# A transformer block on one core: a region of its own for the down weights, late weights on two DMA queues, smaller first loads, one more slot and a new unit order

## The chip, the cores and the metric

The kernel runs on one core of one Trainium2 chip. The metric is the device time of one execution in microseconds (us), the median of several runs. The engines are named as in the profile: PE (TensorE matmuls; PEld its weight loads), DVE (VectorE), ACT (ScalarE), POOL (GpSimd) and SP (SyncE, which here only issues DMAs). DMAs are issued by SP and by ACT, each into a queue of its own; all of them run on the core's 16 DMA engines.

## The reference

One sequence of S = 2048 rows and D = 640 columns goes through linear attention with a softmax feature map, and then through a bilinear gated MLP (F = 1536). All tensors are bf16.

```python
H, Dh = 32, 20
xn = layernorm(x)
q, k, v = split_heads(xn @ wqkv)                      # each [H, S, 20]
phi = lambda t: concat([softmax(t @ w_phi), softmax(-(t @ w_phi))])   # per head, 40 features
kv  = sum over s of phi(k)[s, f] * v[s, d]            # [H, 40, 20]
z   = sum over s of phi(k)[s, f]
o   = (phi(q) @ kv) / (phi(q) @ z + 1e-6)
h   = x + o @ wo
hn  = layernorm(h)
out = h + ((hn @ w_gate) * (hn @ w_up)) @ w_down
```

## The kernel before

The 2048 rows are 16 tiles of 128 rows, numbered t = 0 to 15. The program is a graph of about a thousand operations, and each of them has a name made of a stage and a tile. These are the stages, in the order in which one tile goes through them:

- `x` loads the rows. `L1s`, `L1a`, `L1l`, `L1e` and `L1n` compute the first layernorm's statistics on DVE, ACT and POOL, and `xn` (DVE or ACT) writes the normalised tile.
- `xt` turns that tile, so that its columns lie on partitions. Tiles 0 to 3 are turned by PE and copied out of PSUM by `xte`; the others by a DMA transpose that SP issues (line 468).
- `V`, `K` and `Q` are the three projections on PE (line 481, 10 matmuls of 320 columns). For tiles 0 and 1 they are split into five units each (`K0_0` to `K0_4`), one for each 128-row chunk of the weight. The feature map w_phi is folded into the K and Q weights first: `WT` turns chunk i of wk on PE (line 389), `WTe` copies it out, `F1_i` multiplies it with w_phi (line 408), and `Fe1_i` copies the result into `Wp`. `wqt` and `F0_i` do the same for wq.
- `Kx` and `Qx` are two exponentials each on ACT (line 493), of the projection and of its negative; `Ks` and `Qs` sum them per head on DVE (line 497); `Kr`, `Ke`, `Qr` and `Qe` form the reciprocals on ACT; `Kn` and `Qn` multiply on POOL (lines 517, 549 and 553).
- `KV` adds the tile's share of kv and z on PE (line 525) in one PSUM group over all 16 tiles. `KVe` copies the sum out when all tiles are in.
- `qT` turns the Q features (11 blocks of 128) by a DMA transpose that SP issues (line 560). `N` multiplies them with kv and z (line 578, 12 matmuls); `dd`, `rd` and `o` divide on DVE.
- `oT` turns the quotient by a DMA transpose on SP (line 598). `O` multiplies it with wo (line 604, 10 matmuls), and `h` adds x on DVE.
- `L2s`, `L2a`, `L2v` and `L2r` are the second layernorm's statistics; `hc` centres the tile on ACT or DVE; `hT` turns it by a DMA transpose on SP (line 631).

The MLP runs over five blocks of rows: 256, 512, 512, 512 and 256. `U b_f_g` multiplies block b with the f-th 128 columns of w_gate (g = 0) or w_up (g = 1), 5 matmuls of 256 or 512 columns (line 646). `g` copies the gate out of PSUM on ACT (line 651), and `u` multiplies it with the up product on DVE (line 654). `D` multiplies with the down weights `Wd` (line 665, 24 matmuls of 320 columns for a tile), `y` adds h on DVE (line 677), and `w` stores the tile (line 679). The last tile's `D` is cut into three column ranges. Ten matmuls on zeros (`warm0` to `warm9`, line 368) come first on PE.

The work's order isn't decided at run time. `PLAN` lists, for each operation, a number to sort by, then a choice of engine (empty or 0: the first of its alternatives, 1: the second), then the slots that its result takes in a rotating buffer: `xn4:17.845::0` is operation `xn4`, sorted at 17.845, on its first engine, into slot 0. `arrange` sorts by that number, and each engine then carries out its own list in order. `emit` places the semaphore waits that the data and the reuse of slots need. An instruction that waits therefore holds up all that stands behind it on its engine, DMA issues included. The figures for duration that `G.op` also takes play no part in the emitted program; only the list does.

The rotating buffers of `NSLOTS` include `ph` (4 slots, Q features before turning), `phT` (5, after), `oT` (4) and `psum` (8 banks). `phT` and `oT` lie in one region, `scratch`, where wk and the turned weights lie earlier.

The weights load as follows. `wk` and `wv` (each five chunks of 128 rows, 160 KB a chunk) come in pieces of 2, 2 and 1 chunks at the start, beside `x`, on both queues. After the last `xt`, SP issues `wg` and `wu` (5 pieces of 384 KB each) and `wo` (320 and 480 KB). The down weights are four pieces `wd0` to `wd3` of 480 KB. Their tile `Wd` lies over `Wp`, which holds the folded K and Q weights and the V weights, so they wait for projections:

```python
    for k in range(4):
        dma("sp", "wd%d" % k, ..., key=310, after=kvprojs if k < 3 else projs)
```

`kvprojs` are all K and V projections and `projs` all projections, Q too. In the emitted order SP issues wd0 to wd2 just before the qT of tile 2, and wd3 after the last Q projection.

Of the kernel before, what the change touches and what calls it, by code (L numbers as in the profile page):

```python
# [6 lines left out]
BF16 = mybir.dt.bfloat16  # L7
# [37 lines left out]
NSLOTS = {"psum": 8, "xn": 4, "ek": 7, "va": 8, "SR": 4, "ph": 4, "phT": 5, "o": 3, "oT": 4, "gt": 4, "hh": 2, "out": 3,  # L45
# [3 lines left out]
x0:1.18 wk0:1.66 wk2:1.18:1 wk4:3.1:1 x1:0.7 wv0:1.66 wv2:2.14 wv4:2.62 x2:2.14:1 x4:2.62 x6:3.1 w5:0.7 x8:3.58:1 x10:4.06 x12:3.58 x14:4.06:1  # L49
wqt0:37.137 wqt1:29.337 wqt2:35.837 wqt3:34.537 wqt4:42.509 wo0:50.109 wo2:52.989 wg0:48.669 wu0:47.709 wg1:48.189 wu1:52.029 wg2:52.509 wu2:49.629  # L50
wg3:49.149 wu3:51.549 wg4:51.069 wu4:50.589 id0:0.7 gl0:1 eps:3.13 id1:1.25 gla0:2.69 glb0:5.289 gla4:2.47 glb4:2.91 gla1:3.55 glb1:3.99 gla2:4.41
glb2:5.509 gla3:3.33 glb3:3.77 va1:1.65 phz:6.843 mk0:4.21 mk1:7.743 mk2:8.143 mk3:8.543 mk4:8.943 zero:0.7 warm0:1.08::0 warm1:1.51 warm2:1.94
warm3:2.37 warm4:2.8 warm5:3.23 warm6:3.66 warm7:4.09 warm8:4.52 warm9:4.74 Ph0:5.729 Ph1:6.388 Ph2:4.63 WT0:7.595::0 WTe0:8.469:1 WT1:7.001::3
WTe1:7.55 WT2:6.404::1 WTe2:7.093:1 WT3:6.125::0 WTe3:6.674 WT4:11.659::4 WTe4:12.387:1 F1_0:9.442::6 Fe1_0:10.534:1 F1_1:9.018::4 Fe1_1:9.911
F1_2:7.874::6 Fe1_2:8.609:1 F1_3:7.28::4 Fe1_3:7.985 F1_4:13.296::4 Fe1_4:13.881:1 L1s0:5.222 L1a0:6.542 L1s1:3.734 L1a1:4.734 L1s2:8.887 L1a2:11.457
L1s3:9.707 L1a3:11.347 L1s4:10.527 L1a4:15.165 L1s5:11.567 L1a5:12.805 L1s6:12.915 L1a6:15.055 L1s7:14.235 L1a7:15.275 L1s8:16.205 L1a8:23.367
L1s9:22.547 L1a9:23.587 L1s10:17.025 L1a10:23.477 L1s11:15.385 L1a11:18.345 L1s12:32.127 L1a12:34.367 L1s13:31.307 L1a13:35.897 L1s14:26.537
L1a14:27.857 L1s15:36.007 L1a15:38.247 L1l0:6.832 L1e0:7.262 L1l1:5.024 L1e1:5.454 L1l2:12.009 L1e2:12.439 L1n2:12.949 L1n3:12.749 L1l4:15.95
L1e4:16.794 L1n4:17.304 L1n5:17.704 L1n6:17.104 L1n7:17.504 L1l8:24.71 L1e8:26.417 L1n8:26.955 L1n9:26.755 L1n10:29.714 L1n11:27.155 L1l12:38.83
L1e12:39.29 L1n12:39.901 L1n13:42.86 L1n14:40.101 L1n15:42.66 xn0:7.969::0 xt0:8.739::1 xte0:9.288 xn1:6.042::0 xt1:6.722::2 xte1:7.362 xn2:13.735::1  # L60
xt2:14.434::1 xte2:15.327 xn3:13.162:1:0 xt3:14.154::0 xte3:14.704 xn4:17.845::0 xt4:18.525 xn5:18.14:1:1 xt5:19.825 xn6:19.477:1:2 xt6:21.125
xn7:19.875::3 xt7:22.425 xn8:29.387::1 xt8:31.937 xn9:27.357::0 xt9:28.037 xn10:30.264:1:3 xt10:33.237 xn11:29.55:1:2 xt11:30.637 xn12:40.529::0
xt12:41.209 xn13:44.357::0 xt13:45.109 xn14:40.557:1:1 xt14:43.809 xn15:43.01:1:2 xt15:46.409 V0_0:10.3::0 V0_1:10.572 V0_2:11.115 V0_3:11.387
V0_4:11.938 Ve0:12.539::1 K0_0:13.024::2 K0_1:13.611 K0_2:14.713 K0_3:14.984 K0_4:15.528 Kx0_0:16.17::0 Kx0_1:17.517 Ks0:18.455::0 Kr0:20.814
Ke0:21.677 Kn0:22.037 KV0:25.308::4,5 V1_0:8.195::2 V1_1:8.467 V1_2:9.757 V1_3:10.029 V1_4:10.844 Ve1:11.385::0 K1_0:12.209::6 K1_1:12.481 K1_2:12.753
K1_3:13.883 K1_4:15.256 Kx1_0:16.894::1 Kx1_1:18.854 Ks1:21.127::1 Kr1:23.074 Ke1:23.937 Kn1:24.396 KV1:29.698 V2:17.158::0 Ve2:20.375:1:3
K2:19.874::6 Kx2_0:21.827::3 Kx2_1:24.087 Ks2:25.117::0 Kr2:27.914 Ke2:29.4 Kn2:29.914 KV2:32.73 V3:15.799::4 Ve3:20.19::2 K3:18.516::2
Kx3_0:21.054::2 Kx3_1:22.45 Ks3:23.697::2 Kr3:25.554 Ke3:26.517 Kn3:27.355 KV3:33.046 V4:21.233::4 Ve4:23.314::4 K4:30.014::0 Kx4_0:32.614::5
Kx4_1:33.477 Ks4:34.477::3 Kr4:37.194 Ke4:38.68 Kn4:40.301 KV4:42.87 V5:22.591::0 Ve5:24.93::5 K5:25.623::6 Kx5_0:27.29::0 Kx5_1:28.154 Ks5:29.887::2
Kr5:31.6 Ke5:32.464 Kn5:32.824 KV5:44.544 V6:26.982::0 Ve6:28.777::1 K6:23.949::2 Kx6_0:25.794::4 Kx6_1:26.667 Ks6:27.967::1 Kr6:33.237 Ke6:34.1  # L70
Kn6:35.183 KV6:44.859 V7:31.372::6 Ve7:34.25::0 K7:28.34::2 Kx7_0:30.977::1 Kx7_1:31.84 Ks7:32.947::0 Kr7:34.874 Ke7:35.737 Kn7:37.542 KV7:45.49
V8:37.436::2 Ve8:39.777:1:3 K8:34.72::0 Kx8_0:36.57::3 Kx8_1:37.434 Ks8:38.357::1 Kr8:39.957 Ke8:40.407 Kn8:43.06 KV8:46.435 V9:40.153::6
Ve9:41.781:1:6 K9:38.795::0 Kx9_0:41.27::6 Kx9_1:42.104 Ks9:42.937::0 Kr9:44.537 Ke9:45.4 Kn9:47.778 KV9:51.456 V10:36.078::6 Ve10:38.057::2
K10:41.511::2 Kx10_0:43.723::5 Kx10_1:44.777 Ks10:45.61::1 Kr10:47.21 Ke10:47.66 Kn10:50.137 KV10:53.673 V11:43.185::0 Ve11:44.857:1:4 K11:33.361::2
Kx11_0:35.114::2 Kx11_1:35.947 Ks11:36.827::2 Kr11:39.05 Ke11:39.5 Kn11:45.419 KV11:54.26 V12:55.119::2 Ve12:56.747:1:0 K12:50.097::6 Kx12_0:51.886::3
Kx12_1:52.719 Ks12:53.637::1 Kr12:55.237 Ke12:56.101 Kn12:57.605 KV12:60.552 V13:57.835::0 Ve13:59.464:1:1 K13:48.424::2 Kx13_0:50.052::1
Kx13_1:50.886 Ks13:52.217::0 Kr13:54.023 Ke13:54.886 Kn13:55.246 KV13:63.584 V14:66.616::6 Ve14:68.977:1:0 K14:46.751::6 Kx14_0:48.379::0
Kx14_1:49.212 Ks14:50.046::2 Kr14:51.646 Ke14:52.509 Kn14:52.869 KV14:70.691 V15:67.975::2 Ve15:69.603::1 K15:56.477::6 Kx15_0:58.105::5 Kx15_1:58.939
Ks15:60.215::0 Kr15:62.279 Ke15:63.142 Kn15:65.048 KV15:71.007 KVe0:71.852 KVe1:71.592 F0_0:45.805::0 Fe0_0:46.39 F0_1:45.175::6 Fe0_1:45.76
F0_2:46.12::2 Fe0_2:47.03:1 F0_3:49.782::0 Fe0_3:51.466:1 F0_4:48.109::0 Fe0_4:48.694:1 Q0_0:51.771::2 Q0_1:52.043 Q0_2:52.314 Q0_3:52.586 Q0_4:52.858  # L80
Qx0_0:53.399::4 Qx0_1:54.263 Qs0:55.096::3 Qr0:56.934 Qe0:57.384 Qn0:59.964::0 qT0:62.656::0 Q1_0:53.129::0 Q1_1:53.401 Q1_2:53.988 Q1_3:54.575
Q1_4:54.847 Qx1_0:55.477::2 Qx1_1:56.311 Qs1:57.499::2 Qr1:59.562 Qe1:60.012 Qn1:62.506::1 qT1:65.198::1 Q2:59.194::2 Qx2_0:60.822::6 Qx2_1:61.655
Qs2:62.489::1 Qr2:64.599 Qe2:65.462 Qn2:67.407::0 qT2:71.043::2 Q3:62.226::6 Qx3_0:63.975::4 Qx3_1:64.839 Qs3:65.672::2 Qr3:67.872 Qe3:68.735
Qn3:69.949::1 qT3:72.641::3 Q4:69.333::0 Qx4_0:70.961::6 Qx4_1:71.939 Qs4:72.772::2 Qr4:74.407 Qe4:75.275 Qn4:77.575::0 qT4:80.683::2 Q5:65.258::0
# [152 lines left out]
def build_graph():  # L237
# [665 lines left out]
```

## Time and profile before

| | |
|---|---|
| median of three runs | 278.77 us (278.11 to 279.57) |
| the profiled execution: time, span | 279.31 us, 277.6 us |
| mean granted TensorE clock | 0.994 |
| PE busy | 267.5 us (96%) |
| DVE, ACT, POOL busy | 169.7 us (61%), 113.4 us (41%), 89.8 us (32%) |
| chain that ended last | PE 86%, DMA 7%, DVE 3% |
| HBM read, written | 11.00 MB, 2.62 MB |

Times in the profile count from the first instruction of the span. The execution's own time is 1.7 us more than its span, and this execution was 0.5 us above the median. In a timeline row the columns are start, duration, engine, line, operation, output and inputs, count, and in brackets how long the engine had been idle before the row and what ended that. A row with a count merges successive instructions of one kind. SPq and ACTq rows are DMA issues, and their duration is that of the issue, not of the transfer; the time from issue to landing stands in the DMA rows, after the size. In a row of the windows view the columns are the window, its length, the busy time of PE, PEld, DVE, ACT and POOL (with the number of instructions), the granted PE clock, the share of the DMA engines' time and GB/s.

### The profile page before, as it was taken

Reading aid. Unit: us, or ns where it says so; the run is one execution under the profiler, and the core shown is the slowest. Engines: PE = TensorE matmul, PEld = TensorE weight load, DVE = VectorE, ACT = ScalarE, POOL = GpSimd, SP = SyncE. Lnnn points to the kernel's source line nnn. Section 1 sums busy time; section 2 is a strip of 40 time slices with the busy share of each in tenths; the row PEclk is TensorE's granted clock in tenths of the full one; section 3 lists DMA queues with packets and bytes.
Section 4 is the critical chain, followed back from the end, with each engine's and each line's share of the span. In section 5 each row is a group of like instructions: output and inputs, shape, how many; then the busy total and the mean of one; then the engine's idle time right before and its main releaser. Section 6 shows DMA issues by size and latency. Waiting matters only on the chain.

```text
span 277.6 us, 5213 instructions
## 1 busy us (share of the span) xinstructions
PE 267.5 (96%) x2119; PEld 178.3 (64%) x2119; DVE 169.7 (61%) x317; ACT 113.4 (41%) x240; POOL 89.8 (32%) x107
## 2 busy tenths in 40 slices
PE   7899999999997799999999999999999999999996
PEld 3777778777765577755556787764545457644775
DVE  4899997888778869896734348950244302505323
ACT  2899998769783534443204032213031300013000
POOL 8017999899968507443000000000000000000000
PEclk9999999999999979999999999999999999999999
DMA  7914545996599989867410003550001001100011
GB/s 225 367 38 86 94 100 103 282 399 128 192 203 171 157 160 176 152 90 137 85 24 0 26 24 50 108 108 24 0 24 20 6 12 50 47 0 0 26 47 61
DMA packets 66520, 27.77 MB, mean 100 GB/s; under 512 B 57664, under 2 KB 65216, under 8 KB 66496
## 3 DMA queue, kind: packets, MB, share of 16 engines
q1 hardware_dynamic: 64704, 25.30, 41.2%
q10 hardware_dynamic: 1792, 2.13, 2.3%
q8 instruction: 17, 0.28, 0.4%
q14 instruction: 7, 0.06, 0.1%
HBM read 11.00 MB, written 2.62 MB: 49 GB/s over the span
## 4 chain that ended last, share of the span: by engine, by line
PE 86%; DMA 7%; DVE 3%; ACT 1%; issue 1%; SPq 0%
PE ps L646 35%; PE ps L481 21%; PE ps L665 19%; PE ps L604 6%; DMA scratch<-o 3%; DMA scratch<-in_A_wqkv_dram 2%; PE ps L525 2%; DVE SR L497 1%; PE ps L578 1%; PE ps L408 1%; DMA xnT<-xn 1%; ACT ek L493 1%; DVE o L594 1%; ACT xn L627 1%; DVE ev L654 0%
## 5 line engine op out<-in xcount | busy, mean ns | idle before, releaser
L646 PE MATMUL ps<-xnT,Wgu 128*128 128x512 bf16 (+1 forms) x600 | 108.0, 340 | 0.6 <-DMA xnT<-xn 0.6
L646 PEld LDWEIGHTS ps<-xnT,Wgu 128*128 128x128 bf16 x600 | 59.3, 99 | 45.7 <-DVE ev L654 1.0
L651 ACT ACTIVATE gt<-ps 128x512 bf16<-128x512 f32 (+1 forms) x60 | 30.5, 512 | 108.0 <-PE ps L646 76.8
L481 PE MATMUL ps<-Wp,xnT 128*128 128x320 bf16 x480 | 68.9, 299 | 0.0
L654 DVE TENSOR_TENSOR ev<-ps,gt 128x512 bf16<-128x512 f32 (+1 forms) x60 | 33.0, 578 | 49.4 <-ACT gt L651 19.0
L481 PEld LDWEIGHTS ps<-Wp,xnT 128*128 128x128 bf16 x480 | 45.6, 98 | 16.6
L665 PE MATMUL ps<-Wp,ev 128*128 128x320 bf16 (+2 forms) x396 | 53.2, 295 | 0.0
L493 ACT ACTIVATE ek<-ps 128x640 bf16<-128x640 f32 x64 | 43.4, 701 | 11.1 <-PE ps L481 11.0
L497 DVE TENSOR_REDUCE SR<-ek 128x64 f32<-128x1280 bf16 x32 | 46.7, 1468 | 2.0 <-ACT ek L493 1.4
L665 PEld LDWEIGHTS ps<-Wp,ev 128*128 128x128 bf16 x396 | 38.1, 98 | 14.6 <-issue 0.2
L549 POOL TENSOR_TENSOR ph<-ek,SR 128x1200 bf16<-128x1200 bf16 x16 | 35.5, 2222 | 16.8 <-ACT SR L502 12.7
L517 POOL TENSOR_TENSOR ek<-ek,SR 128x1280 bf16<-128x1280 bf16 x16 | 37.4, 2360 | 5.2 <-ACT SR L502 5.2
L677 DVE SCALAR_TENSOR_TENSOR Wp<-ps,rs,x_all 128x640 bf16<-128x640 f32 (+3 forms) x18 | 14.6, 809 | 31.5 <-PE ps L665 31.4
L618 POOL TENSOR_SCALAR ln<-mv 128x1 f32<-128x1 f32 x16 | 3.3, 210 | 90.0 <-DVE mv L617 89.7
L604 PE MATMUL ps<-Wo,scratch 128*128 128x320 bf16 x160 | 24.1, 299 | 2.5 <-DMA scratch<-o 2.5
L604 PEld LDWEIGHTS ps<-Wo,scratch 128*128 128x128 bf16 x160 | 15.2, 98 | 9.1 <-DMA scratch<-o 3.6
L608 DVE TENSOR_TENSOR x_all<-ps,x_all 128x640 bf16<-128x640 f32 x16 | 13.1, 817 | 5.1 <-PE ps L604 5.0
L594 DVE TENSOR_TENSOR o<-ps,sm 128x640 bf16<-128x640 f32 x16 | 12.9, 815 | 2.8 <-DMA scratch<-o 2.6
L627 ACT ACTIVATE xn<-x_all,mv 128x640 bf16<-128x640 bf16 x12 | 9.9, 825 | 11.1 <-DVE mv L617 10.7
L500 ACT ACTIVATE SR<-SR 128x64 f32<-128x64 f32 x32 | 8.2, 256 | 5.3 <-DVE SR L497 5.3
L578 PE MATMUL ps<-KVm,scratch 128*128 128x63 bf16 x192 | 7.8, 189 | 2.1 <-DMA scratch<-ph 2.1
L578 PEld LDWEIGHTS ps<-KVm,scratch 128*128 128x128 bf16 x192 | 7.3, 98 | 3.7 <-DMA scratch<-ph 2.5
(52 smaller groups left out, 148.9 us busy)
## 6 DMA issues: line engine op xcount, KB each, us to landing
out_dram<-Wp SPq DMA_DIRECT2D x15, 160.0 KB, 1.8
Wgu<-in_B_w_up_dram SPq DMA_DIRECT2D x5, 384.0 KB, 7.6
Wgu<-in_B_w_gate_dram SPq DMA_DIRECT2D x5, 384.0 KB, 6.2
Wp<-in_B_w_down_dram SPq DMA_DIRECT2D x4, 480.0 KB, 5.2
x_all<-in_A_x_dram SPq DMA_DIRECT2D x5, 320.0 KB, 10.1
Wp<-in_A_wqkv_dram ACTq DMA_DIRECT2D x2, 320.0 KB, 6.2
x_all<-in_A_x_dram ACTq DMA_DIRECT2D x2, 320.0 KB, 9.6
Wo<-in_A_wo_dram SPq DMA_DIRECT2D x1, 480.0 KB, 8.9
```

What stands on the lines that cost most here:

```text
L481: ins = e.matmul(pb(b, hb)[:, 0:320], lhsT=T["xnT"][:, NC - 1 - c, P * t:P * (t + 1)], rhs=T["Wp"][:, POS[kind], c, 320 * hb:320 * (hb + 1 ...
L493: G.op("act", "%sx%d_%d" % (nm, t, s), lambda e, s=s, b=b, ek=ek: e.activation(out=T["ek"][:, ek.slots[0], :].rearrange("p (b h s f) -> p ...
L497: G.op("dve", "%ss%d" % (nm, t), lambda e, ek=ek, sr=sr: e.tensor_reduce(out=T["SR"][:, sr.slots[0], 0, :], in_=T["ek"][:, ek.slots[0], :] ...
L517: G.op("pool", "Kn%d" % t, lambda e, ek=ek, sr=sr: e.tensor_tensor(out=T["ek"][:, ek.slots[0], :].rearrange("p (h f) -> p h f", f=DH), in0 ...
L549: e.tensor_tensor(out=o_[:, 0:10 * P].rearrange("p (g n) -> p g n", n=P)[:, :, 0:120].rearrange("p g (h f) -> p g h f", f=DH), in0=i_[:, 0 ...
L578: ins = e.matmul(pb(b, y)[:, 21 * (h0 - 16 * y):21 * (h1 - 16 * y)], lhsT=T["phT"][:, phT.slots[0], g, :], rhs=T["KVm"][:, h0:h1, :].rearr ...
L594: G.op("dve", "o%d" % t, lambda e, sm=sm, b=b, o=o: e.tensor_tensor(out=T["o"][:, o.slots[0], :].rearrange("p (b h d) -> p b h d", b=2, d= ...
L604: ins = e.matmul(pb(b, hb)[:, 0:320], lhsT=T["oT"][:, oT.slots[0], c, :], rhs=T["Wo"][:, c, 320 * hb:320 * (hb + 1)], start=(c == 0), stop ...
L646: ins = e.matmul(pb(b)[:, 0:n], lhsT=T["Wgu"][:, gu, c, P * ft:P * (ft + 1)], rhs=T["xnT"][:, NC - 1 - c, o0:o0 + n], start=(c == 0), stop ...
L651: G.op("act", "g%d_%d" % (bi, ft), lambda e, pg=pg, gt=gt, n=n: e.activation(out=T["gt"][:, gt.slots[0], 0:n], in_=pb(pg)[:, 0:n], func=AF ...
L654: o_ = G.op("dve", "u%d_%d" % (bi, ft), lambda e, pu=pu, gt=gt, hh=hh, ft=ft, n=n: e.tensor_tensor(out=T["hh"][:, hh.slots[0], ft, 0:n], i ...
L665: ins = e.matmul(pb(b, hb)[:, 0:w], lhsT=T["hh"][:, hh.slots[0], ft, P * tt:P * (tt + 1)], rhs=T["Wd"][:, ft, c0 + w * hb:c0 + w * (hb + 1 ...
```

## The change

- `Wd` gets a region of its own (15,360 bytes a partition); the three `out` slots move to the start of `Wp`. The loads wd0 to wd3 then wait for nothing, and they stand among the other late weights in the list.
- The late weights `wo`, `wg`, `wu` and `wd` may go out on SP or ACT. In the new list `wg1`, `wu2` and `wd0` are on ACT.
- `wk` and `wv` load in single chunks of 160 KB, and tiles 2 and 3 of x load one by one. At the start ACT has w5, wk0, wk2, wk4, x3, wv0, wv2 and wv4, between its first activations; SP has x0, wk1, x1, x2, wk3, wv1, x4, wv3, x6 and so on.
- `phT` has six slots instead of five.
- The list is new from end to end: the order on every engine, the choices of engine and the slots. The operations and their shapes are otherwise the same.

Parts of the new order, as read from the list:

| | before | after |
|---|---|---|
| PE, head | WT3 WT2 xt1 WT1 F1_3 WT0 F1_2 V1_0 V1_1 xt0 F1_1 F1_0 ... | WT0 WT1 xt0 WT2 F1_0 F1_1 WT3 F1_2 WT4 K0_0 K0_1 F1_3 V0_0 ... |
| SP, late weights | xt12 wqt4 xt14 xt13 xt15, then wu0 to wo2 | xt15 wg0 xt13 wo0 wu1 wu4 wo2 wd3 xt14 wu3 wg3 wu0 wg2 wd2 wg4 wd1 |
| POOL, Q features | Qn0 Qn1 Kn15 Qn2 Qn3 Qn15 Qn5 Qn4 Qn6 Qn9 ... | Qn1 Qn3 Qn0 Kn14 Qn2 Qn5 Qn6 Qn4 Qn15 Qn9 ... |
| SP, middle | qT0 qT1 wd0 wd1 wd2 qT2 qT3 qT15 oT1 qT5 oT0 qT4 oT2 qT6 oT3 qT9 hT1 hT0 ... | qT1 qT3 qT0 qT2 qT5 oT1 oT0 qT6 qT4 oT2 qT15 oT3 qT9 hT1 hT0 ... |
| PE, middle | N1 Q9 N0 Q8 Q10 Q11 N2 N3 Q7 O1 O0 N5 Q13 O2 Q12 N6 N15 O3 N4 N9, then U0 | N1 N0 Q11 Q12 Q13 N2 Q14 N3 Q10 O1 O0 N5 Q8 N6 O2 Q7 N15 O3 N9 N4, then U0 |
| PE, first D | after U1 and N12, beside U4 | D0 and D1 between U0 and U1 |

```diff
-NSLOTS = {"psum": 8, "xn": 4, "ek": 7, "va": 8, "SR": 4, "ph": 4, "phT": 5, ...
+NSLOTS = {"psum": 8, "xn": 4, "ek": 7, "va": 8, "SR": 4, "ph": 4, "phT": 6, ...
 PLAN = {}
-x0:1.18 wk0:1.66 wk2:1.18:1 wk4:3.1:1 x1:0.7 wv0:1.66 wv2:2.14 wv4:2.62 x2:2.14:1 x4:2.62 x6:3.1 w5:0.7 x8:3.58:1 ...
+x0:0.7 w5:1.18:1 wk0:1.66:1 wv0:5.98:1 wk1:2.14 wv1:5.5 wk2:3.1:1 wv2:6.46:1 wk3:4.06 wv3:7.9 wk4:4.54:1 wv4:7.42:1 ...
...
-    xload("sp", 0, 1, -100)
-    for n_, (a, b_) in enumerate(((0, 2), (2, 4), (4, 5))):
-        dma("sp", "wk%d" % a, lambda a=a, b_=b_: T["wkn"][:, a:b_, :], ...
-        dma("act", "wv%d" % a, lambda a=a, b_=b_: T["Wp"][:, POS[2], a:b_, :], ...
+    for c in range(NC):
+        for k_, nm, dst, bf, kk in ((1, "wk", lambda c: T["wkn"][:, c, :], wkn_b, 1.0), (2, "wv", lambda c: T["Wp"][:, POS[2], c, :], wp_b[2], 2.8)):
+            dma("act" if c % 2 == 0 else "sp", "%s%d" % (nm, c), lambda c=c, dst=dst: dst(c), ...
+    xload("sp", 2, 3, 4.5, also=["act"])
+    xload("act", 3, 4, 4.6, also=["sp"])
...
     def wrows(nm, dst, src, bufs, c0, c1, kb, key):
         return dma("sp", "%s%d" % (nm, c0), lambda: dst()[:, c0:c1, :],
-                   lambda: T[src][P * c0:P * c1, :].rearrange("(c p) n -> p c n", p=P), kb, bufs, key=key)
+                   lambda: T[src][P * c0:P * c1, :].rearrange("(c p) n -> p c n", p=P), kb, bufs, key=key, also=["act"])
...
+    for k in range(4):
+        dma("sp", "wd%d" % k, lambda k=k: T["Wd"][:, 3 * k:3 * k + 3, :], ..., 492, [wd_b[k]], key=102 + k, also=["act"])
...
-    for k in range(4):
-        dma("sp", "wd%d" % k, lambda k=k: T["Wd"][:, 3 * k:3 * k + 3, :], ..., 492, [wd_b[k]], key=310,
-            after=kvprojs if k < 3 else projs)
...
-        T["Wd"] = wp[:, 0:NF * D].rearrange("p (f n) -> p f n", f=NF)
-        T["out"] = wp[:, NF * D:NF * D + 3 * D].rearrange("p (s n) -> p s n", s=3)
+        T["Wd"] = sb([P, NF, D], BF16, "Wd")
+        T["out"] = wp[:, 0:NSLOTS["out"] * D].rearrange("p (s n) -> p s n", n=D)
```

## The prediction

> **What bounds the kernel now.** I read the busy slices first, then TensorE's timeline, then the SP queue's, then the DMA landings by window.
>
> ```profile
> PE   7899999999997799999999999999999999999996
> PEclk9999999999999979999999999999999999999999
> ```
>
> Each slice is 6.94 us. TensorE (PE) has work in all of them but the first two, slices 13 and 14 (83 to 97 us) and the last. Its granted clock dips once, in slice 15. The kernel is bound by PE, so I keep a ledger of PE: lead, work, waits, tail. The timeline names the waits.
>
> ```profile
> 6.81 0.45 PE L459 MATMUL ps<-ident,xn 128*128 128x128 bf16 x5 [0.51 <-DVE xn L450]
> 8.17 0.45 PE L389 MATMUL ps<-ident,scratch 128*128 128x128 bf16 x5 [0.91 <-DMA scratch<-in_A_wqkv_dram]
> ...
> 81.42 0.53 PE L578 MATMUL ps<-KVm,scratch 128*128 128x63 bf16 x12 [0.58 <-DMA scratch<-ph]
> 83.59 1.53 PE L604 MATMUL ps<-Wo,scratch 128*128 128x320 bf16 x10 [0.28 <-DMA scratch<-o]
> 86.61 1.53 PE L604 MATMUL ps<-Wo,scratch 128*128 128x320 bf16 x10 [1.49 <-DMA scratch<-o]
> 96.52 0.53 PE L578 MATMUL ps<-KVm,scratch 128*128 128x63 bf16 x12 [1.50 <-DMA scratch<-ph]
> 97.61 8.39 PE L646 MATMUL ps<-xnT,Wgu 128*128 128x256 bf16 x60 [0.57 <-DMA xnT<-xn]
> 111.35 1.53 PE L604 MATMUL ps<-Wo,scratch 128*128 128x320 bf16 x10 [0.71 <-DMA scratch<-o]
> ```
>
> PE starts its first real unit at 5.48 and ends at 275.23. Waits: 0.51 + 0.91 = 1.42 in the head, 0.58 + 0.28 + 1.49 + 1.50 + 0.57 = 4.42 from 80 to 98, and 0.71 at 111. So 277.6 = 5.48 lead + 263.2 work + 6.55 waits + 2.37 tail. All middle waits are on DMA transposes (qT, oT, hT), which the SP queue issues.
>
> ```profile
> 70.97 1.44 SPq L284 DMA_DIRECT2D Wp<-in_B_w_down_dram  x3
> 72.45 8.38 SPq L560 DMA_TRANSPOSE scratch<-ph  x3
> 80.88 1.28 SPq L598 DMA_TRANSPOSE scratch<-o  x1
> 82.20 1.46 SPq L560 DMA_TRANSPOSE scratch<-ph  x1
> ```
>
> Three down-weight loads (wd0 to wd2, 1.44 MB) go out just ahead of three qT. Those three hold SP 8.38 us. With no load ahead, the 13 transposes from 80.88 to 100.56 take 19.68 / 13 = 1.51 us each, so three would take 4.5. The queue is 3.9 us late from there on. The first of the three landed 7.8 us after its issue:
>
> ```profile
> scratch<-ph SPq DMA_TRANSPOSE x1, 7.8
> ```
>
> against 3.5 to 3.7 for qT elsewhere (windows at 63 and 82). One more effect is the clock:
>
> ```profile
> 92.00:97.60 5.60, 3.54 (x63) 2.80 (x60) 4.38 (x13) 1.93 (x3) 2.90 (x4) 1.00 1.04 138
> 97.60:102.00 4.40, 4.39 (x25) 3.32 (x26) 1.89 (x5) 0.71 (x2) 0.00 (x0) 0.61 0.99 185
> ```
>
> After the two waits before 97.61 the granted clock is 0.61 for 4.4 us. The 60 matmuls of 256 columns there take 8.23 us up to 105.84. Fifteen like them take 1.64 at full clock (112.72 to 114.36), so 60 would take 6.56: 1.67 us lost inside the "work".
>
> **The change, part by part.** The units and their matmuls stay the same, so PE's work stays 263.2, less what the clock gives back.
>
> *Head.* Loads of wk and wv in 160 KB pieces are 10 issues instead of 6, and x2 is split in two: 5 more at about 0.47 us (rows at 0.79 to 2.33). The queues hide them: SP's last load was issued by 5.35 and its loads landed 8 to 11 us after issue. With no such cover they would cost half of 2.3 us, one queue beside the other. What counts is when wk0 to wk4 land. Before, wk0 was 320 KB, third on SP, landed 6.3 us after issue at 8.1, and PE waited 0.91. Now wk0 is second on ACT and wk1 second on SP. By the rows before (185 KB of SP had landed by 5.3, 480 KB of ACT by 5.05) both are there at about 5.3, and the warm-up matmuls hold PE until 5.48 anyway. Then xt0: x0 lands near 3.4, as x1 did before (issue 0.81 + 2.6). From there x1's chain took until 6.81, partly behind other DVE work; about 6.2 now: wait 0.1. WT2 needs wk2 (345 KB on ACT, about 6.7): 0.3. ACT's sequencer issues wk4, x3, wv0, wv2 and wv4 in its own order, between waiting activations, so a late x0 delays them. Queued behind each is the next PSUM eviction. A 0.47 us issue fits under the 0.65 us activation before it, and I add 0.5 for what doesn't. Head waits 0.9 (0.4 to 2.0) instead of 1.42: -0.5.
>
> The Trainium skill, "DMA: Bandwidth & Descriptors", rules for kernel authors, speaks against this part: it asks for at least 1 MiB per DMA and for coalescing, and says that spreading over issuing engines brings no bandwidth. By the row it is half right: two queues moved 330 to 384 GB/s at 3 to 9 us, SP alone 411 GB/s at 56 to 60. By the rule alone this part would gain nothing, and the sum be 0.5 worse.
>
> *Down weights.* Their own region (15 KB a partition) drops the wait for all K, V and Q projections, so wd0 to wd3 go out with the other late weights from about 44 us and not at 71 and 102: wd0 on ACT, wd3 ahead of xt14 on SP, wd1 and wd2 ahead of the first qT. Out of the middle go four issues (1.44 + 0.58 us on SP) and the 3.9 us of blocked queue. They don't vanish: 1.97 MB joins the 4.75 MB loaded from 48 to 63 us. From 44 us at 300 to 400 GB/s the 6.7 MB are through by 61 to 66, so the first qT (63.5 before) may land a few us late; its reader N1 comes ten us later.
>
> *Middle.* Before the first U0 unit PE has the same work in both orders: all projections, nine N, four O. Without waits it would come there at 97.61 - 5.84 + 0.9 = 92.7. It needs hT1 and hT0. In the new order the transposes run qT5, oT1, oT0, qT6, qT4, oT2, qT15, oT3, qT9, hT1, hT0. qT5 needs the fifth feature product on POOL, which ends at 75.6 in the trace of before (rows at 73.12 and 75.30), where POOL had worked without a break from 22.9. So hT0 is issued at 75.7 + 10 x 1.51 = 90.8 and lands, by the rows of oT (2.9) and of hT in this chain (3.7), at 93.7 to 94.5. U0 starts at 94.1 after a wait of 1.4: -3.5 (0 to -4.9). The other readers are later than their transposes: O1 wants oT1 at about 82, oT1 lands at 80.1; O2 wants oT2 near 87, it lands at 86.2.
>
> *Clock.* One wait of 1.4 us: the row at 86.61 shows 1.49 us with no loss of clock. I take -1.7 (0 to -1.7). The Trainium skill, "TensorE: Matmul & The Clock Gate", says that the clock falls after an idle window of about 3.4 us. The row shows it falling after waits of 1.50 and 0.57 with 0.53 of work between; by the rule the loss had another cause and would stay, and the sum be 1.7 worse.
>
> *111 us.* The wait of 0.71 was for an oT behind the late queue: -0.7 (0 to -0.7).
>
> *Late weights on ACT.* wg1, wu2 and wd0 are three issues of 0.45 to 0.6 us at about 44 to 47, where ACT is busy 4.17 and 3.31 of 5 us: hidden; 1.5 if not. ACT also gets one more PSUM eviction (0.71) and one weight copy (0.70) ahead of 40 us, where it is busy 24.2 of 25: +0.3 (0 to 1.4).
>
> *xt13 and xt14* are now behind weight loads on SP. xt13 has 0.39 MB ahead and as much beside it on ACT. xt14 has 2.5 MB ahead and 1.3 beside: 3.8 MB from 43.8 us at 330 to 400 GB/s, plus 2.7 for itself, is 56 to 58; K14 wants it at about 59.6. +0.2 (0 to 3.3).
>
> *Six slots of turned features* only let qT go earlier: 0. The *tail* ends in a 192-column eviction (0.42) instead of 128 (0.35): +0.1.
>
> Sum: -0.5 - 3.5 - 1.7 - 0.7 + 0.3 + 0.2 + 0.1 = -5.8. That lists each wait at its likeliest; a whole new order will add one that I don't see, and I charge 0.5 for it, less than any middle wait but one: -5.3. The span would be 272.3 and the profiled execution 279.3 - 5.3 = 274.0. That execution was 0.5 above the median, so against 278.8 the forecast is 273.5.
>
> **The rivals.**
>
> *The waits only move* (0.20). The transposes themselves set the pace, at 1.51 us each with the DMA engines full (share 1.04 in the window above). If POOL comes 2 us later to the fifth product, hT0 lands at 96.1, PE waits 3.4 us, and the clock falls again: -0.5 - 1.5 - 0.7 + 0.6 = -2.1, or 276.7. For it: that share. Against it: POOL's first product should start as before, at 22.9.
>
> *Slower: xt14 stuck behind the weights* (0.11). Rows for loads beside transposes show 146 GB/s (48 to 49) and 231 (48 to 52). At 231, xt14 lands at 62.9 and PE waits 3.3 at K14; at 180, between those rows, it lands at 67.6 and PE waits 8.0, and the clock falls too, 1.7. It decides from a wait of about 5 us, since 5.0 + 1.7 is more than the gain and the bound below; at 180 GB/s the result is 273.5 + 9.7 - 0.2 = 283.0. Against it: 405 GB/s from 55 to 60.
>
> *It does nothing* (0.07): the down loads block xt as they did qT, and as much is lost there as won: 278.8.
>
> **How the numbers follow.** Forecast 0.62, with its own range 271.5 (every middle wait and the clock gone: -4.9 - 1.7 - 0.7) to 275.3. Adding the first rival reaches 277.6; what lies outside is the second rival, most of the third and a little below: some 2 in 10. This kernel's measurement tells about 0.5%, 1.4 us, from no change. Faster by more than that (under 277.4): 0.82, forecast and first rival; within it 0.06; slower 0.12.
>
> **What would show it.** Right: qT rows near 3.6 us at 70 to 80, no wait on ph or o above 1 us from 80 to 92, U0 starting at 93 to 95 instead of 97.6, clock 1.00 throughout, 60 matmuls of U0 at 0.109 us each. Head: first WT at 5.5 and under 1.2 us of waits before 12. Wrong: a PE wait on xnT at 50 or at 59 to 67 (second rival), U0 after 96 with a low clock (first), or new waits between 12 and 70, where PE has none now.

## The result, and the profile after

The changed kernel takes 277.38 us (median of 20 runs, 276.51 to 280.78), and the kernel before, on the same chip, 279.24 us (278.11 to 280.76). The ratio is 0.9951, interval 0.9928 to 0.9974: faster by some 1.4 us, where 5.3 were forecast. The two medians lie 1.86 apart, the means of the runs that count as fast, all but one, 1.37. The profiled execution took 276.56 us, with a span of 274.8.

The page of the changed kernel, PE's slices and clock, and the DMA rows:

```profile
PE   7899999899999799999999999999999999999995
PEclk9999999999999999999999999999999999999999
GB/s 167 317 144 95 98 110 174 302 294 341 141 147 176 146 141 186 163 74 160 52 47 49 26 0 2 84 50 48 25 2 48 0 0 50 52 0 2 24 48 57
q10 hardware_dynamic: 688, 1.28, 1.9%
```

The dip of the clock is gone in this execution. The 14th slice (89 to 96 us) is still not full, and the eighth (48 to 55) is a new gap. PE's timeline names the waits:

```profile
8.25 0.45 PE L391 MATMUL ps<-ident,scratch 128*128 128x128 bf16 x5 [0.65 <-DMA scratch<-in_A_wqkv_dram]
12.97 2.62 PE L483 MATMUL ps<-Wp,xnT 128*128 128x320 bf16 x18 [0.42 <-DMA Wp<-in_A_wqkv_dram]
53.04 5.61 PE L483 MATMUL ps<-Wp,xnT 128*128 128x320 bf16 x40 [1.30 <-DMA xnT<-xn]
92.27 1.53 PE L601 MATMUL ps<-Wo,scratch 128*128 128x320 bf16 x10 [0.16 <-DMA scratch<-o]
94.08 0.89 PE L575 MATMUL ps<-KVm,scratch 128*128 128x63 bf16 x24 [0.28 <-DMA scratch<-ph]
96.01 9.45 PE L643 MATMUL ps<-xnT,Wgu 128*128 128x256 bf16 x85 [1.04 <-DMA xnT<-xn]
```

Head waits are 1.31 in all, the middle's 0.16 + 0.28 + 1.04 = 1.48 instead of 4.42, and the one at 111 is gone. But U0 starts at 96.01, not 94.1. The wait at 53 is for xt13, the transpose of tile 13, which landed 8.0 us after its issue (2.6 for a pair with no loads about it, in the combined kernel below). In the trace of POOL, VectorE's last rows, and SP's queue:

```profile
57.44 4.67 POOL L519 TENSOR_TENSOR ek<-ek,SR 128x1280 bf16<-128x1280 bf16 x2 [1.50 <-ACT SR L504]
62.06 2.22 POOL L550 TENSOR_TENSOR ph<-ek,SR 128x1200 bf16<-128x1200 bf16 x1
271.46 1.21 DVE L674 SCALAR_TENSOR_TENSOR Wp<-ps,rs,x_all 128x640 bf16<-128x640 f32 x2 [3.19 <-DMA out_dram<-Wp]
76.72 2.47 SPq L561 DMA_TRANSPOSE scratch<-ph  x1
49.65 4.66 SPq L470 DMA_TRANSPOSE xnT<-xn  x1
```

POOL idled 1.50 behind tile 13 and came to its first Q product at 62.06 instead of 60.97. The issue of xt14 alone held SP for 4.66, and xt14 landed after 10.9, yet PE didn't wait for it. At the end y13 waited for a result slot instead of for its matmuls.

The ledger after: 274.8 = 5.12 lead + 262.1 work + 4.28 waits (4.09 named, 0.19 in gaps of a tenth or so) + 3.28 tail.

### The profile page after: what moved, and what is told of

Same layout as the page of the kernel before. It is cut to its first block, busy times and chain, and to the rows that moved or that the text cites. A ratio compares the mean times of both kernels' runs of the same rounds, so it can differ in the third digit from the quotient of the medians.

```text
span 274.8 us, 5227 instructions
## 1 busy us (share of the span) xinstructions
PE 266.0 (97%) x2119; PEld 176.7 (64%) x2119; DVE 172.3 (63%) x319; ACT 113.2 (41%) x240; POOL 88.6 (32%) x105
## 3 DMA queue, kind: packets, MB, share of 16 engines
q10 hardware_dynamic: 688, 1.28, 1.9%
## 4 chain that ended last, share of the span: by engine, by line
PE 84%; DMA 7%; DVE 4%; SPq 3%; issue 0%; DVEq 0%; ACT 0%
PE ps L643 34%; PE ps L483 22%; PE ps L662 17%; PE ps L601 7%; DMA xnT<-xn 3%; SPq L284 2%; PE ps L575 2%; DMA Wp<-in_A_wqkv_dram 2%; DMA scratch<-o 2%; DVE SR L499 2%; PE ps L527 1%; DMA out_dram<-Wp 1%; DVE o L591 1%; SPq L595 0%; DVE Wp L674 0%
## 5 line engine op out<-in xcount | busy, mean ns | idle before, releaser
L643 PEld LDWEIGHTS ps<-xnT,Wgu 128*128 128x128 bf16 x600 | 58.0, 98 | 44.2 <-DVE ev L651 1.2
L662 PE MATMUL ps<-Wd,ev 128*128 128x320 bf16 (+2 forms) x396 | 53.2, 295 | 0.0
L662 PEld LDWEIGHTS ps<-Wd,ev 128*128 128x128 bf16 x396 | 38.2, 98 | 14.9
L624 ACT ACTIVATE xn<-x_all,mv 128x640 bf16<-128x640 bf16 x10 | 8.2, 825 | 16.5 <-DVE mv L614 16.5
L427 DVE BATCH_NORM_STATS2 st<-x_all 128x6 f32<-128x320 bf16 x16 | 7.7, 479 | 3.1 <-DMA x_all<-in_A_x_dram 3.0
## 6 DMA issues: line engine op xcount, KB each, us to landing
Wd<-in_B_w_down_dram SPq DMA_DIRECT2D x3, 480.0 KB, 10.9
```

Source lines behind the costliest of these rows:

```text
L643: ins = e.matmul(pb(b)[:, 0:n], lhsT=T["Wgu"][:, gu, c, P * ft:P * (ft + 1)], rhs=T["xnT"][:, NC - 1 - c, o0:o0 + n], start=(c == 0), stop ...
L662: ins = e.matmul(pb(b, hb)[:, 0:w], lhsT=T["hh"][:, hh.slots[0], ft, P * tt:P * (tt + 1)], rhs=T["Wd"][:, ft, c0 + w * hb:c0 + w * (hb + 1 ...
```

## Experiments

Fourteen kernels were run, each beside runs of the kernel before on the same chip. "First Q" is the start of POOL's first Q product, and "lag" is U0's start less that, both from the one profiled execution. That execution was the longest of its kernel's in e1, e3, f1, f2, g3 and g4, and the shortest in f4, g1 and g2, so its times explain the profile better than the median.

| kernel | median us | ratio to before (interval) | first Q | U0 | lag |
|---|---|---|---|---|---|
| before | 279.24 | 1 | 60.97 | 97.61 | 36.64 |
| after | 277.38 | 0.9951 (0.9928 to 0.9974) | 62.06 | 96.01 | 33.95 |
| e1_wd_alone | 278.91 | 0.9973 (0.9946 to 0.9999) | 63.10 | 99.44 | 36.34 |
| g4_before_wd_behind | 282.22 | 1.0097 (1.0069 to 1.0124) | 60.76 | 94.55 | 33.79 |
| h2_before_wd_gap | 276.74 | 0.9905 (0.9868 to 0.9943) | 60.73 | 94.77 | 34.04 |
| e4_wd_late | 280.92 | 1.0032 (0.9999 to 1.0065) | 62.01 | 96.10 | 34.09 |
| e2_xt_first | 277.16 | 0.9917 (0.9887 to 0.9946) | 62.06 | 95.63 | 33.57 |
| f2_act_late | 277.55 | 0.9915 (0.9883 to 0.9948) | 62.29 | 96.06 | 33.77 |
| f3_wg0_after | 278.33 | 0.9940 (0.9907 to 0.9973) | 61.65 | 96.96 | 35.31 |
| e3_head_two | 277.63 | 0.9940 (0.9910 to 0.9969) | 64.49 | 98.49 | 34.00 |
| f1_out_slots | 277.78 | 0.9932 (0.9901 to 0.9962) | 66.31 | 100.12 | 33.81 |
| g1_wqt4_early | 276.73 | 0.9903 (0.9869 to 0.9937) | 60.99 | 93.97 | 32.98 |
| h1_wqt4_wd_late | 278.29 | 0.9951 (0.9922 to 0.9980) | 60.92 | 94.88 | 33.96 |
| f4_all | 275.32 | 0.9839 (0.9801 to 0.9877) | 59.71 | 93.24 | 33.53 |
| g3_all_wd_late | 274.94 | 0.9855 (0.9824 to 0.9886) | 60.73 | 94.63 | 33.90 |
| g2_all_wqt4 | 273.83 | 0.9811 (0.9786 to 0.9836) | 59.61 | 93.28 | 33.67 |

The lag has two levels: 36.3 to 36.6 where the down loads go out just ahead of transposes that are due, and 33.0 to 34.1 otherwise, in the old order (g4, h2) as in the new. (f3 is between; POOL idled 0.64 and 0.53 more ahead of its third and fourth Q products.) The rest of U0's start is when POOL gets to that product.

### Where the down loads may stand

**e1_wd_alone**: the kernel before with only the region, and the loads behind the other late weights.

```diff
-wd0:69.603 wd1:70.083 wd2:70.563 wd3:95.733
+wd0:53.2 wd1:53.4 wd2:53.6 wd3:53.8
...                                     # the loads' after= goes, and out moves to the start of Wp
-        T["Wd"] = wp[:, 0:NF * D].rearrange("p (f n) -> p f n", f=NF)
+        T["Wd"] = sb([P, NF, D], BF16, "Wd")
```

> The kernel before, with one part of the change alone: the down weights in their own region, their four loads issued on SP right behind the other late weights (about 54 to 57 us). Order of all else as before. Theory (the loads ahead of three qT hold the SP queue 3.9 us): qT at 70 to 80 us lands in under 5 us, PE waits from 80 to 98 fall from 4.42 to under 1.5 us, U0 starts near 94.5 instead of 97.6, the clock stays at 1.00, the wait of 0.71 at 111 goes; span 272 to 273.5, ratio to before 0.980 to 0.987, better than the whole change. Rival (the new order earned what the change gained, the loads are hidden or the transposes pace themselves): waits move by less than 1 us, ratio 0.996 to 1.002.

Almost nothing was won. The SP queue shows the block moved to the first qT:

```profile
57.29 6.30 SPq L284 DMA_DIRECT2D Wd<-in_B_w_down_dram  x4
65.63 17.04 SPq L560 DMA_TRANSPOSE scratch<-ph  x5
```

The first qT landed 7.8 us after its issue. POOL waited for it, since it frees the slot of the next Q product, and VectorE, which waited 3.36 for POOL, copied the sum of kv out so late that PE waited for that:

```profile
73.49 2.22 POOL L549 TENSOR_TENSOR ph<-ek,SR 128x1200 bf16<-128x1200 bf16 x1 [3.12 <-DMA scratch<-ph]
78.55 0.51 PE L577 MATMUL ps<-KVm,scratch 128*128 128x63 bf16 x12 [2.09 <-DVE KVm L532]
```

U0 came at 99.44.

**g4_before_wd_behind**: the kernel before, old region and old waits, the three loads moved behind hT0.

```diff
-wd0:69.603 wd1:70.083 wd2:70.563
+wd0:95.730 wd1:95.731 wd2:95.732
```

> The kernel before, in its own region and with its own waits, with only the three down loads wd0 to wd2 moved on SP from ahead of qT2 to behind hT0 and oT6 (to where wd3 stands, at about 96). Theory A (those loads blocked SP's queue by 3.9 us, and that made the middle's waits of 4.42 us and the clock dip): the three qT are issued in 4.5 to 5 us instead of 8.4 and land in under 4.5, U0 starts at 93.5 to 95.5 instead of 97.6, the clock stays at 1.00; the transposes behind U0 get 2 to 4 us later and may cost 0.5 to 1.5 near 111. Ratio 0.985 to 0.993. Theory B (POOL's products and the transposes' own pace set the middle, the loads took time that SP would have waited anyway): U0 at 96.5 or later, ratio 0.996 to 1.003.

PE's timeline shows both halves, the gain before U0 and its price behind it:

```profile
94.55 8.31 PE L646 MATMUL ps<-xnT,Wgu 128*128 128x256 bf16 x60 [0.76 <-DMA xnT<-xn]
...
112.67 2.85 PE L604 MATMUL ps<-Wo,scratch 128*128 128x320 bf16 x10 [5.18 <-DMA scratch<-o]
```

U0 is 3.06 earlier, as theory A says: the loads did block the middle. Behind U0 the four loads at 99.22 make the next oT land after 8.7, and PE waits 5.18. The price was put at 0.5 to 1.5. And the granted clock falls once more behind that wait:

```profile
112.60:116.00 3.40, 3.33 (x14) 1.99 (x15) 0.45 (x1) 0.00 (x0) 2.20 (x2) 0.50 0.93 177
```

With 0.71 in the 4 us after it, that costs some 2.9 us more, an estimate from the two windows. So 3.06 won, 4.47 more of waiting (5.18 against 0.71) and 2.9 of clock come near the 4.1 by which the span grew. The same block costs more where it now stands.

**h2_before_wd_gap**: own region, and the loads directly behind qT1, where SP waits for POOL anyway. In SP's list that is the place that they had, between qT1 and qT2. What is gone is their wait for the projections, which held SP in the kernel before (its waits from 60 to 82 us: total, times, longest):

```profile
SPq L284 <- PE ps L481: 3.7, 1, 3.7
```

```diff
-wd0:69.603 wd1:70.083 wd2:70.563
+wd0:65.70 wd1:65.71 wd2:65.72          # and the region and no after=, as in e1
```

> The kernel before with a region of its own for the down weights, its three loads wd0 to wd2 directly behind qT1 on SP, where SP then waits about 4 us for POOL's next Q features, instead of directly ahead of qT2; wd3 stays at its place near 96. Theory A (what the region buys is a place in SP's list where no transpose is due while the 1.44 MB drain, which take about 3.6 us at 400 GB/s): the loads go out at about 67, qT2 is issued at 71 without being held and lands in under 5 us, U0 starts 33.5 to 34.5 us behind POOL's first Q product instead of 36.6, so near 94.8, and the ratio is 0.986 to 0.993. Theory B (the loads block whatever place they get near the transposes, as at 59 and at 99): U0 36 us or more behind, ratio 0.996 or more.

```profile
63.26 3.72 SPq L560 DMA_TRANSPOSE scratch<-ph  x2
67.03 1.98 SPq L284 DMA_DIRECT2D Wd<-in_B_w_down_dram  x3
70.49 7.18 SPq L560 DMA_TRANSPOSE scratch<-ph  x3
```

The three qT take 7.18 instead of 8.38 and keep up with POOL's products, U0 starts at 94.77, and the ratio is 0.9905. So this part of the change, alone in the old order, is worth as much as the whole change or more. What pays is when the loads go out. Without the wait that is 3.9 us earlier (67.03 instead of 70.97), and they drain while no transpose is due. The region alone does not pay everywhere, as e1 shows.

**e4_wd_late**, **h1_wqt4_wd_late** and **g3_all_wd_late** put the loads back at their old places in the new order: in the changed kernel, in g1 and in f4 (both below).

```diff
-wd0:45.168:1 wd1:51.052 wd2:50.092 wd3:46.332
+wd0:69.603 wd1:70.083 wd2:70.563 wd3:95.733
```

> The changed kernel with one part undone: the four down-weight loads go out on SP where they did before, three just ahead of the qT of tile 2 and one after the last Q projection, into their own region. Theory: the three qT behind them land in 5 to 8 us, PE waits from 80 to 98 rise from 1.5 to 4 us or more, U0 starts after 98.5, the clock falls after it, ratio to before 1.000 to 1.008. Rival (order): U0 at most 1 us later, no clock dip, ratio 0.995 to 0.999; or better, as the weight traffic at 44 to 60 us shrinks and xt13 lands sooner.

> The changed kernel with wqt4 ahead of xt12, and with the down loads back at their old places in SP's list (three among the qT at 70, one near 96). The same pair of places was compared twice with opposite answers: 0.9951 against 1.0032 in the changed kernel, 0.984 against 0.9855 in the combined one. Theory A (in the new order the loads at 70 go out while SP waits for POOL, so their place costs little; what the first comparison showed came from the turned wq before F0): ratio 0.988 to 0.994, U0 33 to 34.2 us behind POOL's first Q product. Theory B (the place at 70 costs some 2 us by itself): ratio 0.996 or more.

> The combined kernel with the four down loads back at their old places in the list of SP (three among the qT at 70, one near 96). Theory A (it is loading them early that makes the middle fast): U0 starts 1.5 to 4 us later than the 93.2 of the combined kernel, and the ratio rises from 0.984 to 0.992 to 0.998. Theory B (the new order of transposes and feature products makes the middle fast, whatever the place of the down loads, since SP waits for POOL between its qT at 70 and has time for them): U0 at 93 to 94.5, the qT behind the loads land in under 6 us, ratio within 0.004 of 0.984.

The middle doesn't care: the lag is 34.09, 33.96 and 33.90. The loads have their own region here, so they wait for nothing and go out between qT's:

```profile
69.78 1.88 SPq L284 DMA_DIRECT2D Wd<-in_B_w_down_dram  x3
73.13 4.46 SPq L561 DMA_TRANSPOSE scratch<-ph  x2
```

These are rows of h1. Between the last load's issue and the next qT's lie 1.47 us here and 1.48 in h2, but 0.04 in the kernel before; that qT is first due when POOL has its features. So it is not the new order that makes the old place harmless, as h2 has the old one. The times still rose by 0.8% (e4 against after), 0.5% (h1 against g1) and 0.2% (g3 against f4; in these two pairs the intervals overlap). The profiles of e4 and h1 show waits of 0.87 + 0.48 and 0.62 + 0.48 near 125, but f2, whose loads are early, has 0.57 + 0.49 there as well. The ratio of h1, 0.9951, falls between its two theories. What the late place costs, and where, stays open.

### The wait for xt13

**e2_xt_first** moves xt14 directly behind xt13 and all late weights behind both, those of ACT to about 47 to 49. **f2_act_late** moves only ACT's three; **f3_wg0_after** only wg0, from ahead of xt13 to behind it.

```diff
-wg1:42.572:1 wu2:43.825:1 wd0:45.168:1
+wg1:46.9:1 wu2:47.4:1 wd0:48.3:1       # f2; in e2 also xt14:43.06 wg0:43.1, wd0 on ACT as here
-wg0:42.572
+wg0:43.06                              # f3
```

> The changed kernel with xt13 and xt14 ahead of all late weights on SP, and the three late weights on ACT issued after them too. Theory (xt13 landed 8.0 us after its issue because of weights ahead and beside it, PE waited 1.30 for it, and POOL's features and the turned tiles came later by as much): xt13 and xt14 land in about 3 us, the PE wait at 53 goes, U0 starts 1 to 1.5 us earlier than 96.0, ratio to before about 0.989 (the change itself 0.995). Rival (the late weights then run later and hold up the first qT instead, or U0 waits for hT by as much more): U0 stays at 95.5 to 96.5, ratio 0.993 to 0.998.

> The changed kernel, with only the three late weights on ACT (wg1, wu2, wd0, 1.28 MB) issued some 3.5 us later, at about 47 to 49 instead of 43 to 45.5. Theory A (xt13 landed late since 1.28 MB moved beside it on the other queue): xt13 lands under 4.5 us after its issue instead of 8.0, and the PE wait of 1.30 at 53 is gone or under 0.4. Theory B (what stands ahead of xt13 in its own queue, wg0 with 0.39 MB, holds it): xt13 still takes 7 to 8 us and the wait stays at 1 us or more. By A the median is 0.5 to 1.3 us under the changed kernel's, by B the same.

> The changed kernel, with only wg0 (0.39 MB) moved from just ahead of xt13 to just behind it on SP; the three weights on ACT stay where they are. Theory A (the traffic beside xt13 from ACT's queue is what delays it): xt13 still lands 6 us or more after its issue and PE still waits 0.8 us or more near 53. Theory B (the load ahead of it in its own queue): it lands in 3 to 4 us and the wait is gone. By A the median stays, by B it is 0.5 to 1.3 us lower.

The landing of xt13 in the changed kernel, and in f2:

```profile
xnT<-xn SPq DMA_TRANSPOSE x1, 8.0
xnT<-xn SPq DMA_TRANSPOSE x1, 3.8
```

In f2 wg0 is still ahead of it, and the wait at 53 is gone. In f3 xt13 took 8.3 with wg0 behind it, and PE waited 0.54 at 52.63, less than the 0.8 that was expected, and 0.69 at 62.32. So it is the 1.28 MB beside xt13, from ACT's queue, that delays it. In e2, too, the wait is gone. But none of the three brings U0 forward: in e2 POOL started at 23.87 after head waits, in f2 it idled 1.76 at 50.65 after a wait for the turned wq, and both reach the first Q product at 62.06 to 62.29 all the same. POOL works almost without a break from 23 on, and each hold that is left ahead of 62 puts U0 off.

### The head

**e3_head_two**: the first loads really on both queues.

```diff
-w5:1.18:1 wk0:1.66:1 wk2:3.1:1 wk4:4.54:1 x3:5.02:1 wv0:5.98:1 wv2:6.46:1 wv4:7.42:1
+w5:1.18 wk0:1.66 wk2:3.1 wk4:3.2 x3:3.3 wv0:3.4 wv2:3.5 wv4:3.6
```

> The changed kernel with its first loads on two queues: w5, wk0, wk2, wk4, x3, wv0, wv2 and wv4 issued by ACT ahead of its first activation, the rest by SP, in the same order otherwise. Theory (one queue issues 160 KB every 0.47 us, and 229 to 311 GB/s from 3 to 10 us show it, where two queues showed 330 to 384): 320 GB/s or more from 3 to 10 us, PE waits before 13 us fall from 1.3 to 0.4 to 0.8, ratio to before 0.992 to 0.993. Rival (queues share the same DMA engines, so two bring nothing): the same rate, the same waits, ratio 0.995.

Head waits fell from 1.31 to 0.19. The median moved by less than the interval. In the profiled execution, the longest of the twelve, the first folding product F0 waited 3.09 at 46.88 for wqt4, the last turned piece of wq, which landed after 6.4, and that wait ate the gain; for the others this is not shown.

### The turned wq

**g1_wqt4_early**: the changed kernel with wqt4 ahead of xt12 on SP. One number changes.

```diff
-wqt4:39.852
+wqt4:37.2
```

> The changed kernel with one DMA moved: the last turned piece of wq (wqt4) goes out on SP just ahead of xt12 instead of just behind it, so some 2 to 3 us earlier. Theory (the first of the folding products F0 waits for this piece in many executions, since the late weights of ACT's queue now run beside it, and that is what spreads the times of the changed kernel): no PE wait on the turned wq near 45, and the times gather at the lower end, median 276.0 to 277.0, ratio to the kernel before 0.988 to 0.992. Cost if the theory is wrong: xt12 is 1.3 us later; V12 and K12 come at 45 or after, so it should not show. Rival (the wait is only one of several and the next takes its place): ratio 0.993 to 0.997, waits of the same sum elsewhere.

```profile
44.94 0.48 PE L410 MATMUL ps<-Phi,scratch 128*128 128x140 bf16 x6
...
93.97 9.45 PE L643 MATMUL ps<-xnT,Wgu 128*128 128x256 bf16 x85 [0.60 <-DMA xnT<-xn]
```

PE waits nowhere between 14 and 91, POOL is at the first Q product at 60.99, U0 starts at 93.97, where the forecast had 94.1, and the span is 273.1. The median, 276.73, shows that this isn't every execution: they run from 274.84 to 278.60.

### The tail

**f1_out_slots**: the last tiles' results in rotating slots.

```diff
-y11_0:255.829::0 y10_0:259.089::0 y12_0:262.349::0 y13_0:265.609::0 y15_1:266.599::1
+y11_0:255.829::1 y10_0:259.089::2 y12_0:262.349::0 y13_0:265.609::1 y15_1:266.599::2
```

> The changed kernel, with the result slots of the last five tiles in rotation (y11 in slot 1, y10 in 2, y12 in 0, y13 in 1, y15_1 in 2) instead of four in slot 0. Theory (the tail's 0.8 us came from y13 waiting for the store of y12 to leave slot 0, and that store was late because an instruction load ran on a DMA engine just ahead of it): y13 starts 2.4 us after y12 ends instead of 3.2 to 4.0, the tail after the last matmul is 2.4 to 2.5 us instead of 3.3, and the median falls by 0.8 to 1.5 us against the changed kernel, a ratio to the kernel before of 0.990 to 0.993. The store behind the instruction load may still land after 3 us, with nobody waiting for it. Rival (the stores themselves, or the last three vector operations, are slower at the end in the new order): tail and ratio stay, 3.3 us and 0.995.

VectorE's last row, and the stores' landing times:

```profile
275.10 1.41 DVE L674 SCALAR_TENSOR_TENSOR Wp<-ps,rs,x_all 128x640 bf16<-128x640 f32 x2 [2.38 <-PE ps L662]
DMA to landing us min/median/max: 1.5/1.8/4.1
```

One store still takes 4.1, and nobody waits for it: the tail is 278.5 - 275.97 = 2.53. The time can't show 0.8 us (0.9932 against 0.9951, intervals overlapping); this profiled execution lost 3.05 at 48.7 to the turned wq.

### All together

**f4_all** joins e2, e3 and f1. **g2_all_wqt4** adds wqt4 ahead of xt12.

```diff
+# e2, e3 and f1 as above; in g2 also wqt4:37.2
```

> The changed kernel with three edits at once: the first loads of wk, wv, w5 and x3 really on both queues; xt13 and xt14 ahead of all late weights on SP and ACT's weights later; the last tiles' result slots in rotation. Theory (POOL's chain of feature products paces the middle: it was 1.1 us late at 62, once by the wait for xt13, once, with that removed, by a late start at 23.9 after the head; so only both together bring it forward): head waits under 0.4 us, no wait at 53, the first Q product on POOL at 60.5 to 61.3 instead of 62.06, U0 at 93.8 to 94.9 instead of 96.0, tail 2.5 us, span 271.5 to 273.0 us, ratio to the kernel before 0.979 to 0.985. Rival (the single gains are each hidden by the next wait, such as the last turned wq piece before F0): span 274.5 or more, ratio 0.990 or more.

> The three edits of the combined kernel (first loads on both queues, xt13 and xt14 ahead of the late weights, result slots in rotation), and wqt4 ahead of xt12. Theory: the wait of 0.48 at 43.7 goes, and the executions around 273.7 us of span come down towards 272: median 274.0 to 274.9, ratio 0.979 to 0.983. Rival: as the combined kernel before, 0.984, since the first Q product on POOL and with it U0 do not depend on F0.

PE's timeline of g2, where only three waits above 0.1 are left:

```profile
90.10 1.53 PE L601 MATMUL ps<-Wo,scratch 128*128 128x320 bf16 x10 [0.22 <-DMA scratch<-o]
...
93.28 8.36 PE L643 MATMUL ps<-xnT,Wgu 128*128 128x256 bf16 x75 [0.94 <-DMA xnT<-xn]
101.85 1.27 PE L643 MATMUL ps<-xnT,Wgu 128*128 128x256 bf16 x10 [0.20 <-DVE o L591]
```

Single edits, e4 apart, gave 0.1% to 0.5% over the changed kernel, and their intervals overlap its own. Together they give 0.9839, and with wqt4 0.9811: 273.83 us, and four executions within 1.2 us of one another. f4 still waited 0.85 in the head, which had been put under 0.4, but POOL began at 21.75 instead of 23.04. The forecast's 273.5 was there to be had, four edits further on.

## Why the prediction was right or wrong

**The direction held, and the mechanism in part.** The waits of the middle fell by 2.94 (forecast 3.02), the one at 111 went, the two profiles' clocks differ by the forecast 1.67, and the loads' block was real: g4 and h2 take 2.6 to 2.9 off the lag. What the forecast gave to loading early belongs to not loading just ahead of a transpose that is due. Once the wait for the projections is gone, the old place blocks nothing ahead of U0, in the new order (e4, h1, g3) or the old (h2).

**Errors of reading.** The head's list was misread: for w5, wk0, wk2, wk4, x3 and wv0, wv2, wv4 the first alternative is ACT, so 1 means SP. All first loads went out on SP; ACT's queue (q10) moved only 1.28 MB, the three late weights. The section on the change says it wrongly, too. The 0.9 of head waits was 1.31. And U0's start of 94.1 already held the 0.5 of the head, which the sum counted again: the terms make -4.8, a span of 272.8. POOL had not worked without a break, either: it had idled 0.54 at 33 and 0.72 at 53.

**The sizes.** Each term against the 277.6 of before; the sums are -4.8 and -2.8:

| term | forecast | measured |
|---|---|---|
| lead and head waits | -0.5 | -0.36 - 0.11 |
| middle waits | -3.0 | -2.94 |
| clock, in the two profiles | -1.7 | -1.67 |
| wait at 111 | -0.7 | -0.71 |
| xt13, xt14 | +0.2 | +1.30 |
| tail | +0.1 | +0.91 |
| ACT, and a wait unseen | +0.8 | 0.19 in small gaps |
| other work of PE | 0 | +0.57, not explained |

Three terms were mis-sized, and the first is the step that failed. *xt13*: "0.39 MB ahead and as much beside it" counted one weight on ACT where three were issued by 45.9, and charged +0.2 for a transpose that landed after 8.0; PE waited 1.30, and POOL, whose times were taken over from before, idled 1.50. *Tail*: only the last eviction was weighed, not that y13 follows y12 into slot 0. *Head*: the waits shrank by 0.11, not 0.5, since all loads stayed on SP. That the row looks right is luck: 0.36 of it are the ten matmuls on zeros, which ended at 5.12 here, but at 5.48 before and in eight of the fourteen other kernels.

The first rival named what then decided, POOL late to its products. The fifth ended at 76.7 instead of 75.6, and the issue of qT5 behind it took 2.47 (the row at 76.72) instead of 1.51. With 0.4 more along the queue hT0 was issued at 93.3 instead of 90.8, landed within 3.0 where 2.9 to 3.7 were assumed, and U0 started 1.9 late. It came at 96.01 against the rival's 96.1, and the median at 277.38 against its 276.7. It was turned down on POOL's first product, which did start as before (23.04 against 22.86); the time was lost on the way. Its clock loss and its wait of 3.4 did not come, since PE had stopped earlier, at 53. Of the second rival the sign at 50 was seen, for xt13; PE never waited for xt14.

**The profile and the median.** The forecast moved one profiled execution to another. That leaves 277.38 - 276.56 = 0.82 by which the changed kernel's profile lies under its median; the wait for wqt4 found in e3, e4, f1 and f2, and gone with g1, is the part that can be named, though none of the changed kernel's other executions was profiled. In 4 of its 20 runs the mean clock was 0.990 to 0.992, and they took 279.01 to 280.78, where the other 16 have a median of 277.19. The profiles of e3 and f1 (0.990, 0.993) show what such an execution can hold: over 3 us of waiting for wqt4 and a granted clock of 0.72 behind it. Another 0.47 is the kernel before, 279.24 here and 278.77 in the three runs: the forecast took off 0.5 for a profile above its median. With 2.0 for the sizes and 0.5 counted twice this makes 3.8 of the 3.9 missed. The clock is the clearest case: of 85 executions of the kernel before in four comparisons, 48 had a mean clock of 0.998 or more (median 279.19) and 37 less (280.23). The profiled one, with 0.994, was of the second kind. The groups lie 1.0 us apart, and the forecast charged 1.7 in every execution.

**The rules weighed.** The Trainium skill, "DMA: Bandwidth & Descriptors", rules for kernel authors, says that spreading over issuing engines brings no bandwidth, and that it only saves issue time. For 160 KB pieces, at 0.47 us an issue, that time shows: in the second slice of the page, one queue moved 317 GB/s (after), two 372 (e3, which differs in that alone), 367 (before) and 370 (f4). "TensorE: Matmul & The Clock Gate", what's actually happening, has the clock fall after an idle window of about 3.4 us. Here single waits of up to 2.09 (e1) left it alone, and 3.05 (f1) and 3.09 (e3) brought it to 0.72 in the windows 48 to 54 and 46 to 52; but 1.25 and 0.76 with 0.53 of work between gave 0.52 in g4, and 1.31 and 0.85 gave 0.57 in h2.

```profile
94.50:98.00 3.50, 3.45 (x17) 2.51 (x18) 1.73 (x4) 0.38 (x1) 0.00 (x0) 0.52 0.94 176
```

That window of g4 begins with U0. In e1 1.50 and 0.60, nearly the pair of the kernel before, left the clock at 1.00. Such a pair may trip the gate and need not.

## What to carry to other kernels

When a load leaves a queue, ask which transposes are due while it drains at its new place: the same 1.44 MB cost some 3 us in front of due transposes (old order), 5 and a dip of the clock behind U0 (g4), and nothing in a gap where the queue waits for another engine (h2). Look at what a load waits for, too: between before and h2 its place in the list is the same, and only a wait is gone. Find the engine that sets when the bound engine can go on (here POOL, busy from 23 to 90), and follow its holds through the whole stretch: fixing one of several holds ahead of it won little, and fixing all won 1.4% over the changed kernel. Before charging an effect of one profiled execution, look in how many executions it occurs.

## What was not expected of the hardware

A transpose suffers from plain loads on the *other* queue: xt13 took 8.0 us with 1.28 MB issued on ACT from 43.04 to 45.9, and 3.8 when these were issued from 49.45 on (f2). Its issue can hold the queue, too: 4.66 for xt14, against 1.2 to 1.3 for most of its kind.

Loading of instructions can delay a store. In the window 268 to 271.5 of the changed kernel the store of y12 took 3.1 instead of 1.8, with one instruction load among the packets:

```profile
q1 hardware_dynamic: 144, 0.16, 13.7%
q8 instruction: 1, 0.02, 1.8%
out_dram<-Wp SPq DMA_DIRECT2D x1, 160.0 KB, 3.1
```

1.8% of 16 engines' 3.5 us is 1.0 us on one of them; in e2 it was 3.0%, or 1.7, and the store took 4.0. In h1, with the same slots, no instruction load lies in the window from 267.5 to 271.5; the store of y12 took 1.8, and y13 waited only for its matmuls. That the load stood ahead of a part of the store fits these numbers, and wasn't isolated.
